# Gate steps moved ahead of the high/low split in the mixture's unit loop, activation loads two units ahead of their split, one extra weight block

## Chip, cores, metric

The kernel runs on one core of one Trainium2 chip. The metric is device time in microseconds of one execution. Before the change the median of 3 runs is 910.09 us (909.3 to 910.9).

## What is computed

Three stages feed each other. A landmark attention (4 batches, 8 heads, 576 positions, head size 64) gives 2304 tokens of 512 features. A wide softplus layer, called the mixture here, follows, and then a layer in which each token goes to one of 8 experts:

```
x  = attention(q, k, v)                                # 2304 x 512
h  = x @ w_in                                          # 2304 x 2048
x  = (maximum(h, 0) + log1p(exp(-abs(h)))) @ w_out     # 2304 x 512
logits = x @ w_gate ; e = argmax(logits)
gate   = softmax(logits)[e] ; eom = 1 / (1 + exp(-(x @ w_output_gate)))
out[t] = gate[t] * eom[t, e] * (maximum(x[t] @ w1[e], 0) @ w2[e])
```

## The kernel before

All matrix products are made in fp32 out of three products of a rounded high part and a low part (high*high, high*low, low*high). So each operand is split once: ScalarE (ACT) copies it to the high part, and VectorE (DVE) subtracts that from the operand to get the low part.

**Stages.** Attention runs from 0 to about 150 us, the mixture from about 136 to 600 us, and the experts from about 592 us to the end. The change lies in the mixture alone.

**Units.** The 2304 tokens are 9 chunks of 256; the 2048 hidden features are 8 pairs of blocks of 128. A *unit* is one pair of hidden blocks for one chunk: 72 units, numbered from 0 in the list `order` (lines 860 to 877). The first 24 (chunks 0, 1 and 2 interleaved) are the *joint stage*, in which the weights are still being prepared; from unit 24 on come chunks 3 to 8, 8 units each. Per unit TensorE (PE) runs `gemm1` (line 635, 24 matmuls into `ps_h`, of which there are two buffers), and then `gemm2` (line 670, 12 matmuls into `acc`) of the unit two before. Between the two stands `softplus` (lines 641 to 661):

- ACT: `t` = abs, `t` = exp, `u`, `l` = ln (lines 649 to 652), then after the sums `gh`, the high part (line 657);
- DVE: the sums `u`, `d`, `l` (lines 654 to 656), then `gl`, the low part (line 659). `d` is the last reader of `ps_h`.

`t`, `u`, `l`, `d` have one buffer each, `gh` and `gl` three.

**Weight steps.** In the joint stage, `units(n)` takes n steps of the generator `weights` (lines 573 to 602). A weight block is 3 steps: the high part on ACT together with the start of the next block's decoding (lines 596, 98), the low part on DVE (line 599), and the rest of the decoding on DVE (lines 100 to 102) with the next load. There are 21 blocks, ordered by when they are needed; `w_in` blocks 12 and 13 (numbers 13 and 14 of the list) are first used by the `gemm1` of unit 16, and 14 and 15 (numbers 17 and 18) by that of unit 19, the odd one of each pair in the second half of its matmuls. Each unit from 1 takes three steps: one after the four ACT operations, one between `gh` and `gl`, one after `gl`. `EXTRA = 0, 5, 8` adds one step at unit 0 and three each at units 5 and 8.

**Activations.** From chunk 3 on, `load_xr` (line 604) loads a chunk's activations by SyncE's (SP's) queue and `split_x` (line 620, through line 107 on ACT and line 108 on DVE) splits them. Both are issued in the same unit: 23 for chunk 3, and the sixth unit of each chunk for the next (line 915).

**Gate steps.** When a chunk's sums are complete, `gate` (line 676) works in ten steps: (1) ACT copies `acc` to `x` (line 679); (3, 5) PE transposes a half (`ps_tr`, line 689) and ACT copies it to `x2t` (line 690); (4, 6) PE makes the logits (`ps_lg`, line 695) and DVE copies them (line 696); (7) eight short DVE operations; (9) the rank, by PE (lines 726, 727), DVE and ACT; (10) DVE, and the store `x_d` by SP (line 751). From unit 27 on two steps are taken per unit: one between `gemm1` and `softplus`, one after `gemm2`. In the last chunk a hook in the middle of each product takes further ones, and after the gate of chunk 7 come the steps of `early` (line 763), which finds the first slots of the expert stage; the first makes `ps_n` (line 767).

The order on every engine is the order in which this code issues (`manual_schedule`, line 853). The unit loop before (the split of the next chunk and the gate's place in it):

```
h = gemm1(p, xs[c], ...)
next(side, None)                    # gate step
gs[i] = softplus(h, units)          # ACT x4, DVE sums, gh, gl
units(...)                          # EXTRA
xs[c + 1] = split_x(load_xr(c + 1)) # p == 5
gemm2(p2, gs.pop(i - LAG), accs[c2])
next(gate) ; next(side, None)       # gate steps
```

Of the kernel before, what the change touches and what calls it, by code (L numbers as in the profile page):

```python
# [12 lines left out]
F32R = DT.float32r  # L13
# [4 lines left out]
ALU = mybir.AluOpType  # L18
# [8 lines left out]
NE, F2 = 8, 1024  # L27
# [3 lines left out]
CH = 256  # L31
NCH = NT // CH
# [9 lines left out]
"""  # L42
NWA = 8
NWO = 3
EXTRA = 0, 5, 8
JOINT = 3
NFIRST = 2
TAIL = 0, 2, 1, 0, 1, 1, 0, 0, 1, 0, 1, 0, 0, 0, 1, 1
# [62 lines left out]
def chain(*gens):  # L111
    for g_ in gens:
        yield from g_
# [3 lines left out]
def moe_nystrom_kernel(ctx: ExitStack, tc: tile.TileContext, q, k, v, w_in, w_out, w_gate, w_ogate, w1, w2,  # L117
                       consts, out):
    nc = tc.nc
# [10 lines left out]
    def cc(name, rows=128):  # L130
        o, n = COFF[name]
        return cst[:rows, o:o + n]
# [313 lines left out]
    osum = gp.tile([128, NTILE + 1, NE], BF16, name="osum")  # L446
    rd = gp.tile([128, NTILE], F32, name="rd")
    rmat = gp.tile([128, NTILE, 128], BF16, name="rmat")
    tri_b = gp.tile([128, 128], BF16, name="tri_b")
    one_b = gp.tile([128, 128], BF16, name="one_b")  # L450
    wg = gp.tile([128, 4, 2 * NE], F32, name="wg")
# [93 lines left out]
    with ExitStack() as mctx:  # L545
# [5 lines left out]
        m3 = pool("m3", 3)  # L551
# [52 lines left out]
        def load_xr(c):  # L604
            if c <= JOINT - 1:
                t = m2.tile([128, 4, CH], F32, tag="x2", name="xr", bufs=3)
                xr = [t[:, :2], t[:, 2:]]
            else:
                xr = [m2.tile([128, 2, CH], F32, tag="deca", name="xr") for _ in range(2)]
            t0 = c * CH  # L610
            while t0 < (c + 1) * CH:
                b, o = divmod(t0, S)
                n = min(S - o, (c + 1) * CH - t0)
                for j in range(2):
                    nc.sync.dma_start(xr[j][:, :, t0 - c * CH:t0 - c * CH + n],
                                      xT_d[b].rearrange("(k p) n -> p k n", p=128)[:, 2 * j:2 * j + 2, o:o + n])
                t0 += n
            return xr

        def split_x(xr):  # L620
            xh = mx_.tile([128, 4, CH], F32R, tag="xh", name="xh")
            xl = mx_.tile([128, 4, CH], F32R, tag="xl", name="xl")
            for j in range(2):
                js = slice(2 * j, 2 * j + 2)
                split_hi_lo(nc, xr[j], xh[:, js], xl[:, js], nc.vector)
            return xh, xl

        def gemm1(p, x, pool=ph, tag="h"):
            ps = pool.tile([128, 512], F32, tag=tag, name="ps_h").rearrange("p (i n) -> p i n", i=2)
            for i in range(2):  # L630
                hi, lo = wcols(whi, 2 * p + i), wcols(wlo, 2 * p + i)
                n = 0
                for kk in range(4):
                    for a, b_ in ((hi, x[0]), (hi, x[1]), (lo, x[0])):
                        nc.tensor.matmul(ps[:, i], a[:, kk], b_[:, kk], start=n == 0, stop=n == 11)  # L635
                        n += 1
                if i == 0:
                    hook()
            return ps

        def softplus(h, units):

            t = sp.tile([128, 2, CH], F32, tag="t", name="t")
            u = sp.tile([128, 2, CH], F32, tag="u", name="u")
            l = sp.tile([128, 2, CH], F32, tag="l", name="l")
            d = sp.tile([128, 2, CH], F32, tag="d", name="d")
            gh = m3.tile([128, 2, CH], F32R, tag="gh", name="gh")
            gl = m3.tile([128, 2, CH], F32R, tag="gl", name="gl")
            nc.scalar.activation(t, h, AF.Abs)
            nc.scalar.activation(t, t, AF.Exp, scale=-1.0)  # L650
            nc.scalar.activation(u, t, AF.Identity, bias=1.0)  # L651
            nc.scalar.activation(l, t, AF.Ln, bias=1.0)
            units(1)
            nc.vector.scalar_tensor_tensor(u, u, -1.0, t, ALU.add, ALU.subtract)  # L654
            nc.vector.scalar_tensor_tensor(d, h, 0.0, u, ALU.max, ALU.subtract)  # L655
            nc.vector.tensor_tensor(l, l, d, ALU.add)  # L656
            nc.scalar.activation(gh, l, AF.Copy)  # L657
            units(1)
            nc.vector.tensor_tensor(gl, l, gh.bitcast(F32), ALU.subtract)  # L659
            units(1)  # L660
            return gh, gl

        def gemm2(p, g, acc):
            for i in range(2):
# [188 lines left out]
        with tc.manual_schedule():  # L853
            xs = {0: x0}
            xr = [load_xr(c) for c in range(1, JOINT)]
            load_w(0)
            gs, accs = {}, {}
            side = iter(())
            np_ = NFF // 2
            order = [(0, p) for p in range(LEAD)]  # L860
            for p in range(np_):
                order += [(0, p + LEAD)] * (p + LEAD < np_) + [(c, p) for c in range(1, JOINT)]
            nj = len(order)
            work = weights()

            HB = {2: (pa, "acc2"), 3: (pb, "tr")}
            fast = [False]

            def hook():
                if fast[0]:  # L870
                    next(side, None)

            def units(n):
                for _ in range(n):
                    next(work, None)

            order += [(c, p) for c in range(JOINT, NCH) for p in range(np_)]
            first = ("acc0", "acc1"), ("acc2", "acc3"), ("tr", "sm")
            for j in (1, 2):
                xs[j] = split_x(xr.pop(0))  # L880
                load_w(j)
            for i in range(len(order) + LAG):
                fast[0] = len(order) - np_ <= i - LAG + 1 < len(order)
                if i == len(order):
                    for _ in side:
                        pass
                    win_ctx.close()
                    rw = ctx.enter_context(tc.tile_pool(name="rw", bufs=1, side="right", reuse_waits="tile"))
                    for j in range(4):
                        raw.append(rw.tile([128, 4, 512], F32, name=f"raw{j}"))  # L890
                    for _ in range(2):
                        ring[0].append([rw.tile([128, 4, 512], F32R, name=f"{n}{len(ring[0]) + 4}") for n in ("hi", "lo")])
                    wk[0] = splits(0, NBASE)
                if i < len(order):
                    c, p = order[i]
                    if i == nj - 1:
                        xr.append(load_xr(JOINT))
                    h = gemm1(p, xs[c], *HB.get(i, ()))
                    if i > nj + LAG:
                        next(side, None)  # L900
                    gs[i] = softplus(h, units if i else int)
                    if i in EXTRA:
                        units(1 if i == 0 else 3)
                    if i == 2:
                        nc.vector.tensor_copy(tri_b, cc("tri"))
                        nc.vector.tensor_copy(one_b, cc("ones"))
                        nc.vector.memset(osum[:, 0], 0.0)
                        nc.vector.tensor_copy(sgn[:, 0], cc("iota")[:1, :NE])
                        nc.vector.tensor_scalar(sgn[:, 1], cc("iota")[:1, :NE], -1.0, None, ALU.mult)
                        for nm, src in ((0, w_gate), (1, w_ogate)):  # L910
                            nc.sync.dma_start(wg[:, :, nm * NE:(nm + 1) * NE], src.rearrange("(k p) e -> p k e", p=128))
                    if i == nj - 1:
                        xs[JOINT] = split_x(xr.pop(0))
                    if p == 5 and JOINT - 1 < c < NCH - 1:
                        xs[c + 1] = split_x(load_xr(c + 1))
                if i >= len(order):
                    xt[i - len(order)] = t_x(i - len(order))
                    wunits(2)
                if i >= LAG:
                    c2, p2 = order[i - LAG]  # L920
                    if p2 == 0:
                        tags = first[c2] if c2 < JOINT else first[c2 % 2]
                        accs[c2] = [(pa if "acc" in t else pb).tile([128, 512], F32, tag=t, name=t) for t in tags]
                    gemm2(p2, gs.pop(i - LAG), accs[c2])
                    if p2 == np_ - 1:
                        ga_ = gate(c2, accs.pop(c2))
                        next(ga_)
                        side = chain(side, ga_)
                        if c2 == NCH - 2:
                            side = chain(side, early())  # L930
                if nj + LAG < i < len(order) + LAG - 1:
                    next(side, None)
            side = chain(side, route())


# [154 lines left out]
```

## Time and profile before

| | |
|---|---|
| median of 3 runs | 910.09 us (909.3 to 910.9) |
| profiled execution, its own time | 910.2 us |
| span of that execution (first to last instruction) | 908.4 us |
| outside the span | 1.8 us |
| PE / DVE / ACT busy in the span | 859.9 / 666.5 / 586.9 us |
| mean granted TensorE clock | 0.988 of full speed |

All durations below come from the one profiled execution. A row of the timeline gives start, duration, engine, line, operation, result and operands; in brackets stands how long the engine was idle before it, and which operation ended that idle time. Matmuls overlap, so their starts say more than their durations.

### The profile page before, as it was taken

What the parts mean: (1) busy time and instruction counts of PE and PEld (TensorE: products, weight loads), DVE (VectorE), ACT (ScalarE), POOL (GpSimd) and SP (SyncE); (2) the same over time, 40 slices, a digit from 0 to 9 for tenths busy, and PEclk for the clock granted to TensorE, in tenths of its full rate; (3) what the DMA queues carried; (4) which work ended last, traced back from release to release, by engine and by line L of the source; (5) the groups of instructions that cost most, each with busy time, mean ns of one, the idle gap of its engine ahead of it and who ended that gap; (6) DMA issues with size and microseconds to landing.
All of it is one profiled execution on the core that took longest, in us unless ns stands there. A gap on an engine that the chain in (4) does not pass through costs nothing.

```text
span 908.4 us, 15419 instructions
## 1 busy us (share of the span) xinstructions
PE 859.9 (95%) x5826; PEld 718.9 (79%) x5826; DVE 666.5 (73%) x1121; ACT 586.9 (65%) x958; POOL 209.5 (23%) x109
## 2 busy tenths in 40 slices
PE   6998987989998999998999998989999999999996
PEld 3665655888997999998899997877888888888885
DVE  0856697999984465556556463668799999999994
ACT  2554565767774655555455554465888888888883
POOL 0001131000000000000000000034666667666662
PEclk9999999999999999999999999999999999999998
DMA  9856555333300000101011000141118369521600
GB/s 222 196 140 183 158 189 166 95 116 97 113 24 24 1 25 1 47 24 47 1 48 47 1 25 1 47 186 59 36 40 292 148 222 366 185 105 35 232 26 33
DMA packets 49516, 90.92 MB, mean 100 GB/s; under 512 B 5471, under 2 KB 32095, under 8 KB 47392
## 3 DMA queue, kind: packets, MB, share of 16 engines
q1 hardware_dynamic: 41408, 74.43, 26.6%
q0 software_dynamic: 3680, 10.78, 3.7%
q10 hardware_dynamic: 4352, 4.72, 1.5%
q8 instruction: 46, 0.75, 0.4%
q14 instruction: 30, 0.25, 0.1%
HBM read 134.46 MB, written 15.48 MB: 165 GB/s over the span
## 4 chain that ended last, share of the span: by engine, by line
PE 68%; DVE 14%; DMA 6%; ACT 6%; issue 4%; POOL 0%; SPq 0%; DVEq 0%; POOLq 0%; ACTq 0%
PE ps_h L635 19%; PE acc L670 15%; PE ps_g L960 10%; PE ps_y L985 9%; DMA raw<-in_moe_w 3%; DVE lo L479 2%; DVE dect L101 2%; PE ps_hT L974 2%; ACT hi L477 2%; PE ps_lg L695 2%; DVE deca L102 1%; PE ps_t L185 1%; PE ps_t L161 1%; DVE l L656 1%; DVE d L655 1%
## 5 line engine op out<-in xcount | busy, mean ns | idle before, releaser
L479 DVE TENSOR_TENSOR lo<-raw,hi 128x1024 fp32r<-128x1024 f32 x129 | 226.3, 1781 | 11.4 <-ACT hi L477 11.1
L477 ACT ACTIVATE hi<-raw 128x1024 fp32r<-128x1024 f32 x176 | 176.9, 1063 | 8.5 <-DMA raw<-in_moe_w 8.1
L635 PE MATMUL ps_h<-xh,whi 128*128 128x256 f32 x512 | 148.1, 289 | 7.7 <-DVE d L655 4.8
L635 PE MATMUL ps_h<-xl,whi 128*128 128x256 f32 x512 | 146.3, 286 | 0.4 <-DVE xl L108 0.4
L635 PE MATMUL ps_h<-xh,wlo 128*128 128x256 f32 x512 | 146.2, 286 | 0.0
L486 POOL DMA_INDIRECT xg<-x_d,gidx x23 | 37.0, 1610 | 444.1 <-ACT t L650 433.1
L479 POOL TENSOR_TENSOR lo<-raw,hi 128x1024 fp32r<-128x1024 f32 x47 | 116.7, 2485 | 35.8 <-ACT hi L477 35.6
L657 ACT ACTIVATE gh<-l 128x512 fp32r<-128x512 f32 x72 | 45.5, 632 | 116.0 <-DVE l L656 116.0
L654 DVE SCALAR_TENSOR_TENSOR u<-u,t 128x512 f32<-128x512 f32 x72 | 49.6, 688 | 83.5 <-ACT u L651 83.4
L635 PEld LDWEIGHTS ps_h<-xh,whi 128*128 128x128 f32 x512 | 99.2, 194 | 13.6 <-DVE d L655 6.1
L670 PE MATMUL acc<-woh,gh 128*128 128x512 f32 x256 | 103.1, 403 | 1.6 <-ACT gh L657 1.6
L670 PE MATMUL acc<-wol,gh 128*128 128x512 f32 x256 | 101.0, 394 | 0.0
L635 PEld LDWEIGHTS ps_h<-xl,whi 128*128 128x128 f32 x512 | 99.2, 194 | 2.2 <-DVE xl L108 0.6
L670 PE MATMUL acc<-woh,gl 128*128 128x512 f32 x256 | 100.8, 394 | 0.0
L635 PEld LDWEIGHTS ps_h<-xh,wlo 128*128 128x128 f32 x512 | 99.4, 194 | 0.0
L659 DVE TENSOR_TENSOR gl<-l,gh 128x512 fp32r<-128x512 f32 x72 | 49.9, 693 | 38.8 <-ACT gh L657 37.0
L985 PE MATMUL ps_y<-hi,woh 128*128 128x512 f32 x184 | 76.7, 417 | 0.2 <-ACT woh L977 0.2
L985 PE MATMUL ps_y<-hi,wol 128*128 128x512 f32 x184 | 73.3, 398 | 1.4 <-DVE wol L978 1.3
L960 PE MATMUL ps_g<-hi,x0l 128*128 128x512 f32 x184 | 73.9, 402 | 0.3
L985 PE MATMUL ps_y<-lo,woh 128*128 128x512 f32 x184 | 72.7, 395 | 0.0
L960 PE MATMUL ps_g<-hi,x0h 128*128 128x512 f32 x184 | 72.1, 392 | 0.0
L960 PE MATMUL ps_g<-lo,x0h 128*128 128x512 f32 x184 | 71.9, 391 | 0.0
(246 smaller groups left out, 1756.6 us busy)
## 6 DMA issues: line engine op xcount, KB each, us to landing
raw<-in_moe_w SPq DMA_DIRECT2D x88, 1024.0 KB
raw<-in_moe_w_in SPq DMA_DIRECT2D x16, 512.0 KB
raw<-in_moe_w_out SPq DMA_DIRECT2D x16, 512.0 KB
x_d<-x SPq DMA_DIRECT2D x9, 514.0 KB
k<-in_k SPq DMA_DIRECT2D x8, 576.0 KB
q<-in_q SPq DMA_DIRECT2D x8, 576.0 KB
v<-in_v SPq DMA_DIRECT2D x8, 576.0 KB
xT_d<-xo ACTq DMA_DIRECT2D x16, 288.0 KB
```

What stands on the lines that cost most here:

```text
L101: nc.vector.scalar_tensor_tensor(t, hi32, -0x80000000, t, ALU.bitwise_and, ALU.bitwise_or)
L477: nc.scalar.activation(w[0][:, us], raw[i][:, us], AF.Copy)
L479: eng.tensor_tensor(w[1][:, us], raw[i][:, us], w[0][:, us].bitcast(F32), ALU.subtract)
L486: nc.gpsimd.indirect_dma_start(out=xg, out_offset=None, in_=src, in_offset=bass.IndirectOffsetOnAxis(ap=gidx[:, s:s + 1], axis=0))
L635: nc.tensor.matmul(ps[:, i], a[:, kk], b_[:, kk], start=n == 0, stop=n == 11)
L654: nc.vector.scalar_tensor_tensor(u, u, -1.0, t, ALU.add, ALU.subtract)
L657: nc.scalar.activation(gh, l, AF.Copy)
L659: nc.vector.tensor_tensor(gl, l, gh.bitcast(F32), ALU.subtract)
L670: nc.tensor.matmul(acc[tt], a[:, i, ts_], b_[f], start=f == 0 and n == 0, stop=f == NFF - 1 and n == 2)
L695: nc.tensor.matmul(pl[:, :2 * NE], xt[tt][:, kk], wg[:, kk], start=kk == 0, stop=kk == 3)
L960: nc.tensor.matmul(ps, a[:, kk], b_[:, kk], start=n == 0, stop=n == 11)
L985: nc.tensor.matmul(y, a[:, kk], b_[:, kk], start=half == 0 and n == 0, stop=half == 1 and n == 11)
```

## The change

`softplus` becomes a generator of four stretches: the four ACT operations, the DVE sums, `gh`, and `gl`. The loop now issues `gemm2` of the unit two before and the gate step behind it between the sums and `gh`. The weight steps keep their three places. `EXTRA` becomes `15, 15, 15`: no extra steps at units 5 and 8, three at unit 15 (unit 0 keeps its one). For chunk 3 the load is issued in unit 21 and the split in unit 22; for later chunks the load is issued in the fourth unit of the chunk before, the split in the sixth, both after the gate's steps.

```diff
-EXTRA = 0, 5, 8
+EXTRA = 15, 15, 15
...
-        def softplus(h, units):
+        def softplus(h):
...
             nc.scalar.activation(l, t, AF.Ln, bias=1.0)
-            units(1)
+            yield
             nc.vector.scalar_tensor_tensor(u, u, -1.0, t, ALU.add, ALU.subtract)
             nc.vector.scalar_tensor_tensor(d, h, 0.0, u, ALU.max, ALU.subtract)
             nc.vector.tensor_tensor(l, l, d, ALU.add)
+            yield
+            gh = m3.tile([128, 2, CH], F32R, tag="gh", name="gh")
+            gl = m3.tile([128, 2, CH], F32R, tag="gl", name="gl")
             nc.scalar.activation(gh, l, AF.Copy)
-            units(1)
+            yield
             nc.vector.tensor_tensor(gl, l, gh.bitcast(F32), ALU.subtract)
-            units(1)
-            return gh, gl
+            yield gh, gl
...
                     c, p = order[i]
-                    if i == nj - 1:
-                        xr.append(load_xr(JOINT))
-                    h = gemm1(p, xs[c], *HB.get(i, ()))
+                    g = softplus(gemm1(p, xs[c], *HB.get(i, ())))
                     if i > nj + LAG:
                         next(side, None)
-                    gs[i] = softplus(h, units if i else int)
-                    if i in EXTRA:
-                        units(1 if i == 0 else 3)
...
-                    if i == nj - 1:
-                        xs[JOINT] = split_x(xr.pop(0))
-                    if p == 5 and JOINT - 1 < c < NCH - 1:
-                        xs[c + 1] = split_x(load_xr(c + 1))
+                    next(g)
+                    if 0 < i < nj:
+                        units(1)
+                    next(g)
...
                 if nj + LAG < i < len(order) + LAG - 1:
                     next(side, None)
+                if i < len(order):
+                    next(g)
+                    if 0 < i < nj:
+                        units(1)
+                    gs[i] = next(g)
+                    if i < nj:
+                        units(1 + EXTRA.count(i))
...
+                    if i == nj - 3 or p == 3 and JOINT - 1 < c < NCH - 1:
+                        xr.append(load_xr(max(c + 1, JOINT)))
+                    if i == nj - 2 or p == 5 and JOINT - 1 < c < NCH - 1:
+                        xs[max(c + 1, JOINT)] = split_x(xr.pop(0))
```

PE issues the same matmuls in the same order in both kernels. Three places show what moves on the other engines.

SP's queue around the load of chunk 6 (`xr`, in pieces of 192 and 64 columns), before and then changed; `x_d` are the gate's stores:

```order
L751 DMA x_d<-x_3665 128x2x514
L751 DMA x_d<-x_4181 128x2x514
L615 DMA xr<-xT_d 128x2x192 x2
L615 DMA xr<-xT_d 128x2x64 x2
L751 DMA x_d<-x_4723 128x2x514
```

```order
L751 DMA x_d<-x_3661 128x2x514
L615 DMA xr<-xT_d 128x2x192 x2
L615 DMA xr<-xT_d 128x2x64 x2
L751 DMA x_d<-x_4177 128x2x514
L751 DMA x_d<-x_4719 128x2x514
```

The load of chunk 6 moves in front of the store of chunk 3's gate.

ACT in units 65 and 66, where the gate of chunk 7 begins, before and then changed (lines 649 to 652 and 657 of before are 647 to 650 and 658 of the change):

```order
L652 ACTIVATE l<-t 128x512 [waits DVE_49]
L657 ACTIVATE gh<-l 128x512 [waits DVE_49]
L679 ACTIVATE x_6256<-acc_5816 128x512 [waits DMAHW3_49,PE_49]
L679 ACTIVATE x_6256<-acc_5817 128x512 [waits PE_49]
L690 ACTIVATE x2t<-ps_tr 128x512 [waits PE_49]
L649 ACTIVATE t<-ps_h 128x512 [waits PE_49,Activation_49]
L650 ACTIVATE t<-t 128x512 [waits Activation_49]
L651 ACTIVATE u<-t 128x512 [waits Activation_49]
L652 ACTIVATE l<-t 128x512 [waits DVE_49]
L657 ACTIVATE gh<-l 128x512 [waits DVE_49]
L690 ACTIVATE x2t<-ps_tr 128x512 [waits PE_49]
```

```order
L650 ACTIVATE l<-t 128x512 [waits DVE_49]
L679 ACTIVATE x_6252<-acc_5812 128x512 [waits DMAHW3_49,PE_49]
L679 ACTIVATE x_6252<-acc_5813 128x512 [waits PE_49]
L658 ACTIVATE gh<-l 128x512 [waits DVE_49]
L690 ACTIVATE x2t<-ps_tr 128x512 [waits PE_49]
L647 ACTIVATE t<-ps_h 128x512 [waits PE_49,Activation_49]
L648 ACTIVATE t<-t 128x512 [waits Activation_49]
L649 ACTIVATE u<-t 128x512 [waits Activation_49]
L650 ACTIVATE l<-t 128x512 [waits DVE_49]
L690 ACTIVATE x2t<-ps_tr 128x512 [waits PE_49]
L658 ACTIVATE gh<-l 128x512 [waits DVE_49]
```

The copies of `acc` (unit 65) and the second `x2t` (unit 66) move in front of `gh`, which waits for DVE's `l`.

DVE in the joint stage at the low part of `w_in` block 13 (number 14 of the list), before (in unit 13) and then changed (in unit 15, with the three extra steps behind it):

```order
L599 TENSOR_TENSOR wlo_2002<-deca,whi_2001 128x4x128
L659 TENSOR_TENSOR gl<-l,gh 128x512
L100 TENSOR_SCALAR dect<-deca 128x512
L101 SCALAR_TENSOR_TENSOR dect<-raw,dect 128x512
L102 SCALAR_TENSOR_TENSOR deca<-raw,dect 128x512
L654 SCALAR_TENSOR_TENSOR u<-u,t 128x512
L655 SCALAR_TENSOR_TENSOR d<-ps_h,u 128x512
```

```order
L599 TENSOR_TENSOR wlo_2002<-deca,whi_2001 128x4x128
L660 TENSOR_TENSOR gl<-l,gh 128x512
L100 TENSOR_SCALAR dect<-deca 128x512
L101 SCALAR_TENSOR_TENSOR dect<-raw,dect 128x512
L102 SCALAR_TENSOR_TENSOR deca<-raw,dect 128x512
L599 TENSOR_TENSOR wol_2070<-deca,woh_2057 128x512
L100 TENSOR_SCALAR dect<-deca 128x512
L101 SCALAR_TENSOR_TENSOR dect<-raw,dect 128x512
L102 SCALAR_TENSOR_TENSOR deca<-raw,dect 128x512
L652 SCALAR_TENSOR_TENSOR u<-u,t 128x512
L653 SCALAR_TENSOR_TENSOR d<-ps_h,u 128x512
```

Numbers 9 to 14 of the list are made two units later than before, 5 to 8 and 15 to 20 one unit later.

## Rows read from the trace of the kernel before

**Rows 1.** The page, part 1: busy time, share of the span, instructions.

```profile
PE 859.9 (95%) x5826; PEld 718.9 (79%) x5826; DVE 666.5 (73%) x1121; ACT 586.9 (65%) x958; POOL 209.5 (23%) x109
```

**Rows 2.** Stretches: length, busy PE, PEld, DVE, ACT, POOL; PEclk; DMA share; GB/s.

```profile
180.00:215.00 35.00, 30.39 (x191) 26.99 (x191) 31.56 (x51) 24.16 (x42) 0.00 (x0) 1.00 0.35 105
272.00:320.00 48.00, 44.75 (x281) 40.47 (x281) 23.12 (x38) 26.82 (x48) 0.00 (x0) 0.96 0.05 12
363.00:410.00 47.00, 47.00 (x322) 43.22 (x321) 27.09 (x65) 25.88 (x46) 0.00 (x0) 1.00 0.10 34
410.00:460.00 50.00, 47.10 (x296) 41.99 (x295) 27.33 (x72) 26.72 (x49) 0.00 (x0) 0.97 0.15 43
```

**Rows 3.** Timeline of PE: rows with an idle gap ahead, 180 to 600 us.

```profile
191.27 0.39 PE L635 MATMUL ps_h<-xh,whi 128*128 128x256 f32 x1 [2.44 <-DVE d L655]
...
210.57 0.39 PE L635 MATMUL ps_h<-xh,whi 128*128 128x256 f32 x1 [2.17 <-DVE d L655]
...
286.73 0.38 PE L635 MATMUL ps_h<-xh,whi 128*128 128x256 f32 x1 [2.83 <-ACT xh L107]
...
430.01 1.07 PE L695 MATMUL ps_lg<-wg,x2t 128*128 128x16 f32 x8 [2.51 <-ACT x2t L690]
...
457.12 0.66 PE L689 MATMUL ps_tr<-cst,x 128*128 128x128 f32 x4 [0.38 <-ACT x L679]
...
553.06 0.66 PE L689 MATMUL ps_tr<-cst,x 128*128 128x128 f32 x4 [1.37 <-ACT x L679]
...
560.61 1.06 PE L695 MATMUL ps_lg<-wg,x2t 128*128 128x16 f32 x8 [1.36 <-ACT x2t L690]
...
572.27 0.17 PE L767 MATMUL ps_n<-osum,one_b 128*128 128x8 bf16 x1 [1.82 <-DVE cd L736]
```

**Rows 4.** Chain that ended last: start, length, piece; two at full clock, two partly at half.

```profile
303.31 2.75 PE acc L670 x12
306.06 2.87 PE ps_h L635 x24
...
431.07 4.31 PE acc L670 x12
...
561.67 4.47 PE ps_h L635 x24
```

**Rows 5.** Timeline of DVE, joint stage: d of units 5, 6, 14, 15; a weight low part.

```profile
181.97 0.69 DVE L655 SCALAR_TENSOR_TENSOR d<-ps_h,u 128x512 f32<-128x512 f32 x1
...
190.52 0.69 DVE L655 SCALAR_TENSOR_TENSOR d<-ps_h,u 128x512 f32<-128x512 f32 x1
...
236.69 0.69 DVE L655 SCALAR_TENSOR_TENSOR d<-ps_h,u 128x512 f32<-128x512 f32 x1
...
238.09 0.68 DVE L599 TENSOR_TENSOR wol<-deca,woh 128x512 fp32r<-128x512 f32 x1
...
242.06 0.69 DVE L655 SCALAR_TENSOR_TENSOR d<-ps_h,u 128x512 f32<-128x512 f32 x1
```

**Rows 6.** Timeline of PE: the start of unit 7's first product.

```profile
183.05 0.28 PE L635 MATMUL ps_h<-x0h,whi 128*128 128x256 f32 x1
```

**Rows 7.** Timeline of SP and ACT at the load and split of chunk 6.

```profile
422.91 0.36 SPq L751 DMA_DIRECT2D x_d<-x  x1
...
423.36 2.44 SPq L615 DMA_DIRECT2D xr<-xT_d  x4
...
428.32 1.15 ACT L107 ACTIVATE xh<-xr 128x512 fp32r<-128x512 f32 x2 [1.60 <-DMA xr<-xT_d]
```

**Rows 8.** Timeline of DVE in the last chunk: a gate operation; gl of unit 67.

```profile
561.92 0.17 DVE L716 TENSOR_REDUCE mx<-lg 128x2 f32<-128x16 f32 x1
...
571.16 0.69 DVE L659 TENSOR_TENSOR gl<-l,gh 128x512 fp32r<-128x512 f32 x1 [0.69 <-ACT gh L657]
```

**Rows 9.** Timeline, unit 34: gl, and the second product's first matmul that needs it.

```profile
358.83 0.69 DVE L659 TENSOR_TENSOR gl<-l,gh 128x512 fp32r<-128x512 f32 x1 [0.70 <-ACT gh L657]
...
365.02 0.40 PE L670 MATMUL acc<-woh,gh 128*128 128x512 f32 x1
```

More of the change, by code (lines that the diff above doesn't have):

```diff
@@ L646, in softplus @@
             d = sp.tile([128, 2, CH], F32, tag="d", name="d")
-            gh = m3.tile([128, 2, CH], F32R, tag="gh", name="gh")
-            gl = m3.tile([128, 2, CH], F32R, tag="gl", name="gl")
             nc.scalar.activation(t, h, AF.Abs)
@@ L895, in moe_nystrom_kernel @@
                     c, p = order[i]
-                    if i == nj - 1:
-                        xr.append(load_xr(JOINT))
-                    h = gemm1(p, xs[c], *HB.get(i, ()))
+                    g = softplus(gemm1(p, xs[c], *HB.get(i, ())))
                     if i > nj + LAG:
                         next(side, None)
-                    gs[i] = softplus(h, units if i else int)
-                    if i in EXTRA:
-                        units(1 if i == 0 else 3)
[L904 to L911, printed above, removed]
-                    if i == nj - 1:
-                        xs[JOINT] = split_x(xr.pop(0))
-                    if p == 5 and JOINT - 1 < c < NCH - 1:
-                        xs[c + 1] = split_x(load_xr(c + 1))
+                    next(g)
+                    if 0 < i < nj:
+                        units(1)
+                    next(g)
                 if i >= len(order):
@@ L932, in moe_nystrom_kernel @@
                     next(side, None)
+                if i < len(order):
[5 more added lines that the diff above has]
+                        units(1 + EXTRA.count(i))
+                    if i == 2:
+                        nc.vector.tensor_copy(tri_b, cc("tri"))
+                        nc.vector.tensor_copy(one_b, cc("ones"))
+                        nc.vector.memset(osum[:, 0], 0.0)
+                        nc.vector.tensor_copy(sgn[:, 0], cc("iota")[:1, :NE])
+                        nc.vector.tensor_scalar(sgn[:, 1], cc("iota")[:1, :NE], -1.0, None, ALU.mult)
+                        for nm, src in ((0, w_gate), (1, w_ogate)):
+                            nc.sync.dma_start(wg[:, :, nm * NE:(nm + 1) * NE], src.rearrange("(k p) e -> p k e", p=128))
+                    if i == nj - 3 or p == 3 and JOINT - 1 < c < NCH - 1:
+                        xr.append(load_xr(max(c + 1, JOINT)))
+                    if i == nj - 2 or p == 5 and JOINT - 1 < c < NCH - 1:
+                        xs[max(c + 1, JOINT)] = split_x(xr.pop(0))
             side = chain(side, route())
```

## The prediction, made before the changed kernel ran

> **What bounds the kernel now.** I read the page first: PE is busy for 95% of the span [rows 1], so time is to be had only where PE stands idle or runs slow. Then the stretches: from 363 to 410 us PE is busy for all 47.00 us, while from 180 to 215 it lacks 4.61 us, from 272 to 320 3.25 us and from 410 to 460 2.90 us [rows 2]. Then the timeline of PE, which names each gap and what ended it [rows 3]. Between 180 and 600 us these are all the places with over 0.3 us: two in the joint stage behind DVE's `d` (2.44, 2.17), one at chunk 3 behind the split (2.83; the whole 3.25 us of that stretch, with a short second wait right behind it), one at 430 behind `x2t` (2.51), one of 0.38 behind a copy of `acc`, and three in the last chunk (1.37, 1.36, 1.82). A unit without a gap takes 2.75 + 2.87 = 5.62 us on PE [rows 4].
>
> **What a gap costs besides itself.** After the gap at 430 the next twelve matmuls took 4.31 us and not 2.75; after that at 560.6 a first product took 4.47 and not 2.87 [rows 4]. That is 1.56 and 1.60 us more, at the lower of the two clock levels, 1.2 instead of 2.4 GHz. The stretch 272 to 320, with the 2.83 us gap, has a granted clock of 0.96 [rows 2], which is 0.04 x 48 = 1.9 us of clock by a rounded figure; I take 1.6. The stretch 180 to 215 with its two gaps stayed at 1.00 [rows 2]. So a gap of 2.5 us may bring a slow stretch or not.
>
> A row and a rule differ here. From 410 to 460 PE's idle time is 2.90 us, but weight loading is busy for 41.99 of 50 us, against 43.22 of 47 where nothing waits [rows 2]; at that rate the stretch has lost 50 - 41.99 x 47/43.22 = 4.3 us. The Trainium skill, "Perfetto Trace Analysis", section "Identifying the Most-Contended Engine", says that matmul busy time is no good measure of the headroom and that the share of weight loading is. By the idle gaps alone the sum below would be 9.7 us, with the slow clock it is 14.5; by that rule the trace sides with the larger.
>
> **Joint stage: no gain.** DVE is the busiest engine there (31.56 of 35 us) [rows 2]. `d` comes every 242.06 - 236.69 = 5.37 us, and 190.52 - 181.97 = 8.55 us across an extra block [rows 5]; PE needs 5.62. So DVE wins 0.25 us per unit on PE, and an extra block costs it 3.2. Before, the block at unit 5 finds no reserve, and neither does that at 8: the two gaps. The change takes both away. `d` of unit 5 ends at 182.66 [rows 5] and unit 7's first product starts at 183.05 [rows 6]; from there the reserve grows to some 2.9 us at unit 15, where one extra block uses it up. That looks like 4.6 us won.
>
> But the weight blocks now come later. Number 14 is made in unit 15 and is needed in the second half of unit 16's first product; 18 in unit 18, needed in unit 19. A block's low part ends 238.77 - 237.38 = 1.39 us after the end of its unit's `d` [rows 5]. The `d` of unit 15 ends at 182.66 + 10 x 5.37 = 236.4, so block 14 is there at 237.8. PE would reach the 15th matmul of unit 16 at 183.05 + 9 x 5.62 + 14 x 0.12 = 235.3. **A new wait of 2.45 us.** The `d` of unit 18 ends 8.55 + 2 x 5.37 later, at 255.7, block 18 at 257.05; PE, 2.45 late, would be there at 183.05 + 12 x 5.62 + 2.45 + 1.68 = 254.6. **A second wait of 2.43 us.** Together 4.88 for 4.61: +0.3 us. A slow stretch after the first would be swallowed by the second, for block 18 sets the time; one after the second would cost 1.6. Bounds: -4.6 (no new wait) and +3 (both waits 0.5 longer, and a slow stretch). I take +0.3. The other blocks are ready in time: number 10 ends 182.66 + 6 x 5.37 + 1.39 = 216.3, and unit 13 wants it at 183.05 + 6 x 5.62 + 1.68 = 218.4.
>
> **Chunk 3's split: -4.85.** Issued in unit 22 and not 23, it runs a unit (5.62 us) earlier on ACT and DVE, and PE's idle time there is 3.25 us [rows 2]; with the slow stretch, 3.25 + 1.6. The load is issued after unit 21's steps, about 11 us ahead of the split's use; the one slow load seen took 428.32 - 423.36 = 5 us from issue to its split [rows 7].
>
> **Chunk 6's load: -4.45.** SP issued it behind the gate's store at 422.91, which waits for DVE; ACT then sat 1.60 us at `xh` [rows 7], and `x2t`, behind it on ACT, held PE for 2.51 [rows 3]. The change puts the load in front of that store and two units ahead of the split, and `x2t` in front of the split. So 2.51 and the slow 1.56 go; so do the 0.38 us at 457, where the copy of `acc` stood behind `gh`. The other loads showed no wait and move with nothing behind them but stores.
>
> **Last chunk: -5.5.** The gaps of 1.37 and 1.36 end when ACT gets to the copy of `acc` and to `x2t` [rows 3], both behind `gh`, which waits for `l`. In front of `gh` they need only PE: both go, with the slow 1.60. The gap of 1.82 waits for DVE's rank step, which stands behind `gl`; `gl` with its wait for `gh` is 0.69 + 0.69 [rows 8]. In the change `gl` comes after that step. Of 1.82 some 0.6 stay (1.82 - 1.38 = 0.44, and a little for the steps of `early`, which DVE cannot start earlier by as much). So 1.37 + 1.36 + 1.2 + 1.6 = 5.5.
>
> **What is pushed back.** `gh` now waits behind ACT's gate copies, which wait for PE, and `gl` behind DVE's gate steps. In a plain unit `gl` ends at 359.52 and is first needed at 365.02 [rows 9], 5.5 us of reserve. The copy of `acc` or `x2t` can start once PE has done 2.75 us of second product [rows 4] and the transposes, about when `l` is ready; the longest gate step puts eight short DVE operations of 0.17 us [rows 8], some 1.4 us, in front of `gl`. ACT's next abs waits for PE's next product anyway. I cost it at nothing; without that cover it would be the 1.4 us of such a unit.
>
> **Sum.** 0.3 - 4.85 - 4.45 - 5.5 = -14.5 us. The profiled execution took 910.2 us, 0.1 above the median of 910.09, so against the median: **895.6 us**. The expert stage starts when the last first product ends and shifts as a whole.
>
> **Rivals.**
>
> - *The new waits in the joint stage cost clock too.* They are as long as the gap that did (2.51) and the one that did not (2.44) [rows 3]. For it: two of them; against: the stage kept clock 1.00 with such gaps [rows 2]. +1.6, and up to 0.5 for each wait: 897 to 899. Chance 0.20.
> - *PE does not wait for the blocks.* The two joint gaps simply go: 895.6 - 4.9 = 890.7. Against it: DVE's 5.37 us rhythm leaves no room. Chance 0.07. The same section of the Trainium skill tells to work on the most contended engine first; that is DVE here by its busy time, and the change takes none of its work away, so by that rule too this rival fails.
> - *Half stays.* The split or the gate's copies meet another wait just behind (the store of a gate held in SP's queue, PSUM of the rank step), and one of the three gains of about 5 us is lost: about 900.5. Chance 0.08.
> - *Slower.* ACT takes its queue in order, so every gate copy in front of `gh` now ties `gh`, `gl` and the next ln (which needs `l`'s one buffer) to PE's second product. It decides if `gl` comes more than a unit (5.62 us) after its time, when ACT and DVE no longer keep PE's rhythm. Priced by the longest step, 1.4 us [rows 8], in two of the five units that each of 7 gates spans: 14 x 1.4 = 19.6 us more, 915. Against it: 5.5 us of reserve [rows 9]. Chance 0.05.
> - *Nothing moves*, since new waits take all back: 910. Chance 0.03.
>
> The forecast has 0.57. It spans 893.5 to 897 (0.5 on each wait, 0.4 on each slow stretch). The range of 8 in 10 takes in the clock rival and half of the third at the top, and the no-wait rival at the bottom: 890.5 to 900.5. A measurement of this kernel can tell about 0.2% (1.8 us) from no change. Faster: all but the last two, 0.92; same 0.03; slower 0.05.
>
> **What would show it.** Gaps of PE at the first products of units 16 and 19, each about 2.4 us, behind DVE's weight low part; none behind `d`. No gap ahead of chunk 3. No ACT wait for `xr`, and no gap at `x2t` or the copies of `acc`. One gap of about 0.6 us at `ps_n`. Slow-clock stretches: from 150 to 600 us none, or one after unit 19. The forecast is wrong if PE waits for `gl` or `gh` anywhere after unit 24, or if the joint stage ends much before or after its old time.

## The result, and the profile after

| | before | after |
|---|---|---|
| median | 909.69 us (908.71 to 910.9, 4 runs) | 896.23 us (895.14 to 896.6, 4 runs) |
| ratio | 1 | 0.9849, 95% interval 0.9832 to 0.9867 |
| profiled execution / its span | 910.2 / 908.4 us | 895.93 / 894.1 us |

The change makes the kernel 13.5 us faster; 895.6 was forecast. In the page, part 1, of the changed kernel, the busy times are those of [rows 1] within 3.2 us for every engine, while the span is 14.3 us shorter. The work is the same; waits and some slow clock have gone.

```profile
PE 856.7 (96%) x5826; PEld 716.9 (80%) x5826; DVE 665.1 (74%) x1121; ACT 587.2 (66%) x958; POOL 209.4 (23%) x109
```

Line numbers in the changed kernel: sums 652 to 654, `gh` 658, `gl` 660, abs 647; from the gate on they are as before. First its stretches (columns as in [rows 2]):

```profile
180.00:215.00 35.00, 35.00 (x225) 31.84 (x224) 32.52 (x53) 26.63 (x46) 0.00 (x0) 1.00 0.31 93
215.00:240.00 25.00, 22.86 (x145) 20.54 (x144) 23.34 (x38) 17.04 (x29) 0.00 (x0) 1.00 0.34 103
240.00:272.00 32.00, 30.07 (x182) 27.09 (x181) 26.05 (x42) 21.85 (x38) 0.00 (x0) 0.95 0.21 60
272.00:320.00 48.00, 48.00 (x315) 43.85 (x315) 24.07 (x40) 30.27 (x53) 0.00 (x0) 1.00 0.06 17
410.00:460.00 50.00, 50.00 (x337) 45.67 (x336) 28.46 (x72) 28.47 (x52) 0.00 (x0) 1.00 0.10 33
```

PE now has no idle time from 180 to 215, from 272 to 320 and from 410 to 460 us, where it lacked 4.61, 3.25 and 2.90 [rows 2]. It lacks 2.14 and 1.93 us in two stretches of the joint stage instead. Then the timeline of PE, all rows with 0.3 us idle ahead or more from 180 to 590 us:

```profile
235.52 0.39 PE L635 MATMUL ps_h<-x0h,whi 128*128 128x256 f32 x1 [0.51 <-ACT whi L596]
237.66 0.38 PE L635 MATMUL ps_h<-x0h,wlo 128*128 128x256 f32 x1 [1.63 <-DVE wlo L599]
254.83 0.39 PE L635 MATMUL ps_h<-x0h,whi 128*128 128x256 f32 x1 [0.30 <-ACT whi L596]
256.96 0.58 PE L635 MATMUL ps_h<-x0h,wlo 128*128 128x256 f32 x1 [1.62 <-DVE wlo L599]
556.94 0.17 PE L767 MATMUL ps_n<-osum,one_b 128*128 128x8 bf16 x1 [0.43 <-DVE cd L736]
561.90 0.24 PE L791 MATMUL ps_i<-erhs,rmat 128*128 128x4 bf16 x4 [0.52 <-DVE erhs L786]
```

All eight rows of [rows 3] are gone but the one at `ps_n`, and that shrank from 1.82 to 0.43. New are the waits for weight blocks in units 16 and 19, 0.51 + 1.63 and 0.30 + 1.62. At `ps_i`, in the last chunk, there is a new wait of 0.52. The chain that ended last shows what the clock took behind the second of the waits for blocks (start, length, piece):

```profile
256.96 2.50 PE ps_h L635 x10
259.46 3.11 PE acc L670 x12
```

The same two pieces behind the same wait (1.63) in a kernel that differs only in when the loads of chunks 4 to 8 are issued (further down), where the stretch 240 to 272 has a granted clock of 1.00:

```profile
256.33 1.45 PE ps_h L635 x10
257.78 2.75 PE acc L670 x12
```

So the lower clock level took 1.05 + 0.36 = 1.41 us, which is in the 0.95 of the stretch 240 to 272. And the idle time is not all that a wait costs: at full clock ten matmuls take 10/24 of 2.87 = 1.20 us [rows 4], but 1.45 behind this wait.

Where the time came from is read from the starts of the units' first products in the two timelines of PE:

| first product of unit | before | after | difference | won or lost since the row above | forecast |
|---|---|---|---|---|---|
| 7 | 183.05 | 182.84 | -0.21 | | |
| 20 (behind the joint waits) | 261.25 | 262.41 | +1.16 | +1.37 | +0.3 |
| 25 (behind chunk 3's split) | 294.65 | 290.51 | -4.14 | -5.30 | -4.85 |
| 48 (behind chunk 6's load) | 442.32 | 433.81 | -8.51 | -4.37 | -4.07 |
| 64 | 538.86 | 529.60 | -9.26 | -0.75 | -0.38 |
| 71 (last chunk) | 588.37 | 573.63 | -14.74 | -5.48 | -5.5 |
| end of the profiled execution | 910.2 | 895.93 | -14.27 | +0.47 | 0 |

On ACT (its timeline), chunk 6's split now follows `gh` with no wait for its load, and in the next unit `x2t` stands in front of `gh` and waits for PE alone:

```profile
421.95 0.63 ACT L658 ACTIVATE gh<-l 128x512 fp32r<-128x512 f32 x1 [0.83 <-DVE l L654]
422.49 1.13 ACT L107 ACTIVATE xh<-xr 128x512 fp32r<-128x512 f32 x2
...
427.48 0.60 ACT L690 ACTIVATE x2t<-ps_tr 128x512 f32<-128x512 f32 x1 [1.53 <-PE ps_tr L689]
427.98 0.62 ACT L658 ACTIVATE gh<-l 128x512 fp32r<-128x512 f32 x1
```

What was pushed back is seen in unit 53, one of those with the least reserve from unit 25 to 69 (unit 61 is 0.04 us tighter). The timelines of DVE and PE, `gl` and the second product's first matmul, before and then changed:

```profile
482.28 0.69 DVE L659 TENSOR_TENSOR gl<-l,gh 128x512 fp32r<-128x512 f32 x1 [0.70 <-ACT gh L657]
...
488.15 0.40 PE L670 MATMUL acc<-woh,gh 128*128 128x512 f32 x1
```

```profile
473.46 0.67 DVE L660 TENSOR_TENSOR gl<-l,gh 128x512 fp32r<-128x512 f32 x1
...
479.04 0.40 PE L670 MATMUL acc<-woh,gh 128*128 128x512 f32 x1
```

`gl` now ends at 474.13, 4.91 us before it is wanted; in the same unit of before it was 5.18. The least of all these units was 4.91 before (unit 62) and is 4.87 now, so the worst case has hardly moved; unit 66, which had 13.03, has 8.46. PE waits for `gl` or `gh` nowhere after unit 24.

### The profile page after: what moved, and what is told of

It reads as the page before. It is cut to its first block, busy times and chain, and to the rows that moved or that the text cites. A ratio compares the mean times of both kernels' runs of the same rounds, so it can differ in the third digit from the quotient of the medians.

```text
span 894.1 us, 15416 instructions
## 1 busy us (share of the span) xinstructions
PE 856.7 (96%) x5826; PEld 716.9 (80%) x5826; DVE 665.1 (74%) x1121; ACT 587.2 (66%) x958; POOL 209.4 (23%) x109
## 4 chain that ended last, share of the span: by engine, by line
PE 69%; DVE 14%; DMA 5%; issue 5%; ACT 4%; POOL 1%; SPq 0%; DVEq 0%; POOLq 0%; ACTq 0%
PE ps_h L635 19%; PE acc L670 16%; PE ps_g L966 10%; PE ps_y L991 9%; DMA raw<-in_moe_w 3%; DVE dect L101 2%; PE ps_hT L980 2%; DVE lo L479 2%; PE ps_lg L695 2%; DVE deca L102 2%; PE ps_t L185 1%; ACT hi L477 1%; PE ps_t L161 1%; PE ps_l L197 1%; DVE d L653 1%
```

## Experiments: what each part is worth

Four kernels ran beside the kernel before, which took 910.64 us there. **The extra block alone**: the kernel before with one line changed.

```
-EXTRA = 0, 5, 8
+EXTRA = 0, 15
```

> The kernel before with only the extra weight blocks changed (none at units 5 and 8, one at unit 15). My theory: the two gaps behind d (2.44 and 2.17 us) go and two waits for a weight block, at the first products of units 16 and 19, come in their place, 2.45 and 2.43 us by the prediction (2.1 and 1.9 in the changed kernel). About 909.7 us, 0 to +1.6 with a slow-clock stretch behind the second. Rival (the gaps simply go): 905.1 us and no wait at units 16 and 19.

Measured: 910.01 us, ratio 0.9991 (0.9976 to 1.0007). No change that can be measured, as the forecast's joint term of +0.3 said: the two gaps behind `d` went, and waits for weight blocks came at unit 16 (0.51 + 1.63) and unit 19 (0.64).

**The loads alone**: the kernel before, with load and split as in the change and `gh` and `gl` where they were.

```
-if i == nj - 1: xr.append(load_xr(JOINT))        # in front of gemm1
-if i == nj - 1: xs[JOINT] = split_x(xr.pop(0))
-if p == 5 and ...: xs[c + 1] = split_x(load_xr(c + 1))
+if i == nj - 3 or p == 3 and ...: xr.append(load_xr(max(c + 1, JOINT)))
+if i == nj - 2 or p == 5 and ...: xs[max(c + 1, JOINT)] = split_x(xr.pop(0))
```

> The kernel before with only the loads and chunk 3's split moved (load two units ahead of the split, chunk 3's split in unit 22); gh, gl and the weight steps stay. My theory: chunk 3's gap with its slow stretch (4.85 us) and chunk 6's (2.51 + 1.56) go, the small gap of 0.38 and those of the last chunk stay: 909.7 - 8.9 = 900.8 us. Rival (the gap at chunk 6 comes from x2t standing behind gh and the split on ACT, not from the late load): only 4.85 goes, 904.8 us, and PE still waits for x2t near 425 us.

Measured: 902.12 us, ratio 0.9913 (0.9889 to 0.9938). The gap at chunk 3 is gone; the one at chunk 6 shrank from 2.51 to 0.81 us. Timelines of ACT and PE in this kernel, where `gh` is line 657:

```profile
420.51 0.63 ACT L657 ACTIVATE gh<-l 128x512 fp32r<-128x512 f32 x1 [1.83 <-DVE l L656]
421.05 1.14 ACT L107 ACTIVATE xh<-xr 128x512 fp32r<-128x512 f32 x2
422.09 0.58 ACT L690 ACTIVATE x2t<-ps_tr 128x512 f32<-128x512 f32 x1
...
422.72 1.06 PE L695 MATMUL ps_lg<-wg,x2t 128*128 128x16 f32 x8 [0.81 <-ACT x2t L690]
```

ACT no longer waits for the load, but `x2t` still stands behind `gh` and the split. So the earlier load takes 1.70 us off that gap, and the place of `x2t` holds the rest (the next kernel shows that this place alone takes off all of it). The gaps of the last chunk stayed.

**The order alone**: the changed kernel with load and split issued in one unit as before and the old extra blocks. Both then stand at the end of that unit, behind `gl` and the gate's steps, so this is not the order quite alone: the loads of chunks 7 and 8 come behind one store more than before.

```
-EXTRA = 15, 15, 15
+EXTRA = 5, 5, 5, 8, 8, 8
-if i == nj - 3 or p == 3 and ...: xr.append(...)    # and the split's line
+if i == nj - 1: ...                                 # chunk 3's load and split, as before
+if p == 5 and ...: xs[c + 1] = split_x(load_xr(c + 1))
```

> Only the new place of gh and gl (behind the second product and the gate step); loads issued with the split as before, chunk 3's split in unit 23, extra blocks at units 5 and 8. My theory: the last chunk's gaps go (5.5 us with the slow stretch), and chunk 6's gap too (4.45), since x2t now stands in front of the split though the load is still late; chunk 3's gap stays: 909.7 - 9.9 = 899.8 us, with an ACT wait of 1 to 2 us for xr near 424 us that PE does not feel. Rival (the late load holds PE all the same): 903.9 us. If the split late in the unit holds chunk 3 longer than before, up to 1 us more.

Measured: 905.28 us, ratio 0.995 (0.9933 to 0.9966), 5.5 us above what I expected. Chunk 6's gap went whole, though ACT still waits 0.92 us for its load; the last chunk's gaps shrank. What I had not seen are two new gaps behind `d` (0.72 and 0.89 us), and that 0.88 and 0.38 stay at a copy of `acc` and at `x2t`: 2.87 us, most of the 3.5 by which the profiled execution (903.33 us) lies above what I expected. The first new one in the timelines of SP, ACT and PE:

```profile
477.76 0.36 SPq L751 DMA_DIRECT2D x_d<-x  x1
478.22 1.34 SPq L615 DMA_DIRECT2D xr<-xT_d  x2
...
481.97 1.34 ACT L107 ACTIVATE xh<-xr 128x512 fp32r<-128x512 f32 x2 [4.69 <-DMA xr<-xT_d]
...
486.79 0.36 PE L635 MATMUL ps_h<-xh,whi 128*128 128x256 f32 x1 [0.72 <-DVE d L653]
```

The load of chunk 7 is here behind the store of chunk 5's gate in SP's queue, and the store waits for DVE; before, it was behind that of chunk 4 (453.64). The split is the last thing that ACT does in the unit, so ACT stands 4.69 us, the next unit's abs and exp come late, DVE's `d` with them, and PE waits. The second new gap follows in the same way from 4.93 us of ACT at chunk 8's load, and ACT has not caught up when the gate of chunk 7 begins: its abs of unit 65 starts 5.13 us after that unit's first product, against 3.13 in the changed kernel. That fits the two gaps that stay, but no run tests it. So the later place of the split needs a load that is not pushed behind the next gate's store.

**Everything but the extra block**: the changed kernel with the old blocks.

```
-EXTRA = 15, 15, 15
+EXTRA = 5, 5, 5, 8, 8, 8
```

> The changed kernel with the extra weight blocks back at units 5 and 8. My theory: the joint stage is bound by DVE's work either way, two gaps of 2.4 and 2.2 us behind d instead of 2.1 and 1.9 behind weight blocks: within 1.6 us of the changed kernel (896.2), so 894.5 to 897. Rival (moving the block was worth its two gaps): 4 to 5 us slower than the changed kernel, 900.5 us.

Measured: 895.38 us, ratio 0.9842 (0.982 to 0.9863): the whole gain without the extra block's move. Its timeline of PE has the two gaps behind `d` of before and no wait for a weight block:

```profile
191.53 0.39 PE L635 MATMUL ps_h<-xh,whi 128*128 128x256 f32 x1 [2.42 <-DVE d L653]
...
210.84 0.39 PE L635 MATMUL ps_h<-xh,whi 128*128 128x256 f32 x1 [0.68 <-DVE d L653]
```

The second is 0.68 and not 2.17, because the lower clock followed the first (0.83 from 190 to 200 us, where it was 1.00 before): PE comes to it later by as much. So waits alone do not tell what the stage costs; the time from the first product of unit 7 to that of unit 20 does. It is 78.20 us before, 78.18 here and 78.17 with the extra block alone.

So the loads and chunk 3's split give 8.5 us by the medians, the order 5.4 beside later loads, the two together 15.3, and the move of the extra block nothing that can be measured. No kernel moved `gh` without `gl`; what each is worth in the last chunk is not shown.

## Experiments: the split's place, and how early the load has to be

The kernel before took 910.17 us beside these two and the two with POOL below. **Chunk 3's split alone back to unit 23**, with its load still at unit 21:

```
-if i == nj - 2 or p == 5 and ...:   # split
+if i == nj - 1 or p == 5 and ...:
```

> The changed kernel with chunk 3's split alone put back from unit 22 to unit 23, behind that unit's gl; its load stays at unit 21. Theory: the split's place on ACT made the gap in front of unit 24, not the load: it comes back at 2.83 + 0.42 us, with 1.6 us of half clock behind it: 896.2 + 4.85 = 901.1 us (899 to 902). Rival: the load's lateness made it, and with the load early the split at unit 23 is hidden: 896.2 us.

Measured: 900.06 us, ratio 0.9892 (0.9869 to 0.9916), outside the changed kernel's interval by little, and outside that of the next kernel, which ran beside it. Timeline of PE and the stretch 272 to 320:

```profile
286.89 0.38 PE L635 MATMUL ps_h<-xh,whi 128*128 128x256 f32 x1 [2.83 <-ACT xh L107]
287.69 0.39 PE L635 MATMUL ps_h<-xl,whi 128*128 128x256 f32 x1 [0.42 <-DVE xl L108]
...
272.00:320.00 48.00, 44.74 (x293) 40.53 (x292) 23.77 (x38) 27.39 (x48) 0.00 (x0) 1.00 0.05 12
```

The gap of before came back to the hundredth with its load early, so the split's place made it. By the medians the price is 3.8 us above 896.23, not 4.85. In this profile no lower clock followed (1.00): the five units from 20 to 25 take 31.88 us, against 28.10 in the changed kernel and 33.40 before. So 3.25 us of idle time cost 3.78, and the lower clock of before 1.52.

**Chunks 4 to 8 loaded one unit ahead instead of two**:

```
-if i == nj - 3 or p == 3 and ...:   # load
+if i == nj - 3 or p == 4 and ...:
```

> The changed kernel with the loads of chunks 4 to 7 one unit in front of their split instead of two. The only transfers that change their order are chunk 6's, which now stand behind the store of 417.3 us instead of in front of it; they would be issued from about 417.7 to 420.2 us and land near 422.5 us, against a split near 424 us. Theory: one unit is enough where the split stands in front of the next unit's work, 896.2 us (895 to 897.5). Rival: a load behind the store lands too late, ACT waits for it and chunk 6's logits with it, at most the 4.45 us that the prediction gave for chunk 6: 898 to 900.7 us.

Measured: 895.89 us, ratio 0.984 (0.9817 to 0.9863): no difference. First the timeline of SP at chunk 6's load. In that of ACT its split waits 0.49 us for it, and PE has no gap there. The last row is the stretch 240 to 272 of the comparison above:

```profile
415.33 0.36 SPq L751 DMA_DIRECT2D x_d<-x  x1
415.79 2.48 SPq L615 DMA_DIRECT2D xr<-xT_d  x4
...
421.03 1.15 ACT L107 ACTIVATE xh<-xr 128x512 fp32r<-128x512 f32 x2 [0.49 <-DMA xr<-xT_d]
...
240.00:272.00 32.00, 30.07 (x190) 27.02 (x189) 26.70 (x43) 23.40 (x42) 0.00 (x0) 1.00 0.23 66
```

From chunk 4 on, every load stands here behind the same store as in the kernel before: chunk 6's behind that of chunk 3's gate, as in [rows 7]. So beside the new order the loads of these chunks need not move in front of any store. What costs time is the place behind the next gate's store that the order alone gave to chunks 7 and 8. One unit is enough for that, and the second unit of the change gains nothing; chunk 3's split is another matter.

## Experiments: can the joint stage's last 4 us be had?

**The low part of a weight block on POOL**, which is idle there, instead of DVE:

```
-nc.vector.tensor_tensor(lo, a, hi.bitcast(F32), ALU.subtract)
+nc.gpsimd.tensor_tensor(lo, a, hi.bitcast(F32), ALU.subtract)
```

> The changed kernel, but the low part of a weight block in the joint stage is taken on POOL instead of DVE; POOL is idle there (0.00 us busy between 180 and 272 us), DVE is busy 23.3 of 25 us between 215 and 240 us. Theory: the two waits left in the joint stage (2.14 us in front of unit 16, 1.92 us in front of unit 19) come from DVE's rate, a low part is 0.69 us of DVE per unit; with it gone both waits go, with the 1.7 us of the half-clock stretch behind the second: 896.2 - 4.06 - 1.7 = 890.5 us (889.5 to 892.5). Rival 1: the waits come from the order of the steps (a block is finished one unit before it is used, whatever DVE's rate), and POOL's low part takes 1.36 us instead of 0.69: each wait grows by about 0.7 us, 897.6 us (896.5 to 899). Rival 2: POOL's use makes DVE's own rows longer, so that the gap returns behind d: 896 us or more.

Measured: 904.9 us, ratio 0.9936 (0.9915 to 0.9957). My theory was 14 us off. Timelines of DVE and POOL in this kernel, unit 9:

```profile
207.07 0.69 DVE L653 SCALAR_TENSOR_TENSOR d<-ps_h,u 128x512 f32<-128x512 f32 x1
207.86 1.10 DVE L654 TENSOR_TENSOR l<-l,d 128x512 f32<-128x512 f32 x1
209.66 0.69 DVE L660 TENSOR_TENSOR gl<-l,gh 128x512 fp32r<-128x512 f32 x1 [0.70 <-ACT gh L658]
...
213.71 1.10 DVE L654 TENSOR_TENSOR l<-l,d 128x512 f32<-128x512 f32 x1
...
207.10 1.31 POOL L599 TENSOR_TENSOR wol<-deca,woh 128x512 fp32r<-128x512 f32 x1 [4.54 <-ACT woh L596]
```

The timeline of DVE in the same unit of the changed kernel:

```profile
204.05 0.69 DVE L654 TENSOR_TENSOR l<-l,d 128x512 f32<-128x512 f32 x1
204.66 0.68 DVE L599 TENSOR_TENSOR wol<-deca,woh 128x512 fp32r<-128x512 f32 x1
205.44 0.69 DVE L660 TENSOR_TENSOR gl<-l,gh 128x512 fp32r<-128x512 f32 x1
...
209.43 0.69 DVE L654 TENSOR_TENSOR l<-l,d 128x512 f32<-128x512 f32 x1
```

There the low part fills exactly the 0.7 us in which `gl` must wait for `gh`. Taken out, it leaves DVE idle for 0.70 us, so nothing is saved; and `l` takes 1.10 instead of 0.69 us while POOL works. From one `l` to the next it is 213.71 - 207.86 = 5.85 us against 209.43 - 204.05 = 5.38. PE needs 5.62, so DVE has turned from 0.24 us ahead per unit to 0.23 behind. Unit 20 starts at 270.53 instead of 262.41, 8.1 us later: about all of the loss. By the rhythm 3.7 us of it are there when unit 16 starts (237.16 against 233.43). The other 4.4 come in unit 16, whose waits are 3.02 + 0.57 instead of 0.51 + 1.63, with the clock at 0.50 behind them from 242 to 247 us. The second rival named the right engine, but not that the saving itself was nil.

**The same with two extra blocks, at units 6 and 12** (`EXTRA = 6, 6, 6, 12, 12, 12`):

> As the kernel with the low parts on POOL, with the extra blocks' steps two at unit 6 and unit 12 instead of one at unit 15, so every block is finished earlier. By DVE's rate as the cause: 890.5 us (889.5 to 892.5), the same as with the one extra block at unit 15, since DVE is no longer full. If the order of the steps is the cause: the waits go here and only here, 890.5 us here against about 897.6 us there. If POOL slows DVE: gaps behind d at the units after 6 and 12, 895 us or more.

Measured: 903.53 us, ratio 0.9931 (0.9911 to 0.995). No wait for a weight block is left, but gaps of 3.81 and 3.56 us behind `d` follow the extra blocks. First products stand 5.85 us apart again from unit 15 to 20: DVE has no reserve.

The kernel before took 910.23 us beside the last four. **The changed kernel again**:

> The changed kernel once more, for comparison with the other kernels of this call: 896.2 us (895 to 897), with waits of 0.51 + 1.63 us for unit 16's weight block and 0.3 + 1.6 us for unit 19's.

Measured: 895.47 us, ratio 0.9838 (0.9814 to 0.9862), with the same waits of 0.53 + 1.63 and 0.31 + 1.63.

**The extra block's three steps at three units, one each**:

```
-EXTRA = 15, 15, 15
+EXTRA = 5, 8, 11
```

> The changed kernel with the one extra block's three steps at units 5, 8 and 11, one step each, instead of all three at unit 15. Theory: in the joint stage a unit is 5.62 us of PE against a loop of 5.38 us through DVE, so DVE gains 0.24 us on PE in each unit; spread out, the steps' 2.5 us of DVE (0.69 + 0.42 + 0.69 + 0.69) meet the reserve three times instead of once, and the block is early, so that the waits of 2.14 and 1.92 us go: gaps of 1 to 2 us behind d are left of 4.06, and no stretch of half clock behind them: 893.5 us (892 to 895.5). Rival: the extra work is 2.5 us of DVE wherever it stands and the reserve is used up by then; the waits turn into gaps behind d of the same sum: 896 us (895 to 897).

Measured: 904.33 us, ratio 0.9934 (0.9912 to 0.9957), 8.9 us slower than the kernel just above. Both theories fall, for both counted DVE's work and not its order. Timelines of DVE and ACT between units 7 and 8 of this kernel:

```profile
201.83 0.69 DVE L102 SCALAR_TENSOR_TENSOR deca<-raw,dect 128x512 int32<-128x512 int32 x1
202.44 0.68 DVE L660 TENSOR_TENSOR gl<-l,gh 128x512 fp32r<-128x512 f32 x1
...
205.60 0.69 DVE L652 SCALAR_TENSOR_TENSOR u<-u,t 128x512 f32<-128x512 f32 x1 [1.68 <-ACT u L649]
...
202.56 0.64 ACT L596 ACTIVATE woh<-deca 128x512 fp32r<-128x512 f32 x1 [1.16 <-DVE deca L102]
...
203.65 0.58 ACT L647 ACTIVATE t<-ps_h 128x512 f32<-128x512 f32 x1
```

A unit has three places for weight steps and a block has three steps, so each step meets the same place in every unit. One step more shifts that: now the decoding stands where the low part stood, and the block's high part stands on ACT in front of the next abs. It waits 1.16 us for the decoding, and DVE then waits 1.68 for ACT. The first products of PE stand 7.15 us apart instead of 5.62, with gaps of 2.41, 1.25, 1.27 and 1.28 us behind `d`, until the second extra step changes the order again. Unit 16's wait is gone, but unit 19's grows to 1.72 + 1.63.

**The same at units 8, 11 and 13**:

> The changed kernel with the extra block's steps at units 8, 11 and 13, one each. By the theory that a spread block is paid from DVE's 0.24 us per unit: later steps find more reserve than at 5, 8 and 11, gaps of 0.5 to 1.5 us, 893 us (891.5 to 895). By the rival that the work is paid in full wherever it stands: 896 us (895 to 897).

Measured: 903.54 us, ratio 0.9923 (0.99 to 0.9946): again gaps of 1.67, 1.27, 1.27 and 1.34 us behind `d`, and a wait of 1.78 + 1.64 for unit 19's block. The shift costs the same later.

**One whole extra block, at unit 5**:

```
-EXTRA = 15, 15, 15
+EXTRA = 5, 5, 5
```

> The changed kernel with the one extra block at unit 5 instead of unit 15. Theory: one gap of 2.4 us behind d at unit 8, as with two extra blocks, and unit 16's wait gone; unit 19's is answered by the same block, so it goes too: 4.06 - 2.4 = 1.6 us less, 894.6 us (893.5 to 896). Rival: a block at unit 5 serves unit 16 alone and unit 19's 1.92 us stays: 896.4 us (895.5 to 898).

Measured: 894.7 us, ratio 0.9833 (0.9808 to 0.9859), which can't be told from the 0.9838 of the changed kernel. Its timeline of PE:

```profile
191.21 0.39 PE L635 MATMUL ps_h<-xh,whi 128*128 128x256 f32 x1 [2.43 <-DVE d L653]
...
257.14 0.39 PE L635 MATMUL ps_h<-x0h,wlo 128*128 128x256 f32 x1 [0.66 <-DVE wlo L599]
```

Unit 16's wait is gone. Unit 19's stays, as the rival said, but shows as 0.66 and not 1.92, since PE comes to it late: the clock fell behind the gap of 2.43 (0.50 from 193 to 196 us), and the wait takes that in. From unit 7 to unit 20 it is 78.19 us. With whole extra blocks and the low part on DVE, wherever the blocks stood (one early, one late, two early), this time is 78.17 to 78.21 in eight profiles, the one before among them. Only the two of the changed kernel, where the lower clock fell behind the last wait and nothing after it could take it in, have 79.57 and 79.66. No placement tried beat the changed kernel measurably.

## Why the prediction was right

**The reading of PE's gaps** carried it. Each gap was named with the operation that ended it and the reason why that was late, and each reason was tested: the split's place (its move back restores 2.83 + 0.42), `x2t` and the copies of `acc` behind `gh` (gone with the order), and the load of chunk 6 behind the store, which turned out not to matter beside the new order.

**Joint stage**, forecast +0.3. The mechanism was right: the new waits stand at units 16 and 19, behind the low part, at 2.14 and 1.92 us where 2.45 and 2.43 were worked out from DVE's rhythm, and with the loads one unit ahead, at full clock, the stage costs what it cost before (78.18 against 78.20). But the first rival came in as well: lower clock followed the second wait, 1.41 us, and the term measured +1.37. That a slow stretch behind the first wait would be swallowed by the second was right too: in the kernel with the extra block alone and in that with chunk 3's split put back, unit 16 took 9.84 and 9.81 us instead of 8.27, unit 19's wait shrank to 0.64 and 0.67, and the stage took 78.17 and 78.18.

**Chunk 3**, forecast -4.85, measured -5.30 to unit 25. The clock's part was about right, 1.52 where 1.6 was taken. The gap was priced too low: 3.25 us of idle time cost 3.78, for the first matmuls behind a gap take longer than those in a stream (with the split put back, the 23 behind the second wait took 3.01 us at full clock, where 23/24 of 2.87 is 2.75).

**Chunk 6**, forecast -4.45, measured -4.37 to unit 48 and -0.75 to unit 64 with the copy of `acc`: -5.12. The idle time and the clock in it were sized right, and what they leave out is again of the size seen behind other gaps. The forecast named two moves for it without parting them, and gave the term to the load. The runs part them: `x2t` in front of `gh` and the split removes the gap with the load still late, the load alone leaves 0.81.

**Last chunk**, forecast -5.5, measured -5.48. `ps_n` kept 0.43 of the 0.6 allowed, and a new wait of 0.52 stands at `ps_i`, later in `early`. Idle time and clock alone would have given 1.37 + 1.36 + 1.39 + 1.60 - 0.52 = 5.20, so the match to 0.02 is partly luck.

**The cover of `gl`**: costed at nothing, rightly; the least reserve is 4.87 us, against 4.91 before.

The errors (-0.21, +1.07, -0.45, -0.67, +0.02, and +0.47 after unit 71) sum to +0.23 in the profile: +1.56 against -1.33. That they offset each other is luck; the total is better than its terms.

The rival without waits for the blocks fell, and the Trainium skill's rule beside it ("Perfetto Trace Analysis", "Identifying the Most-Contended Engine": work on the engine that is busy most) needs care here: DVE is the busiest of its kind, yet taking 0.69 us per unit from it saved nothing, since the way from `l` through ACT's `gh` to `gl` is as long without that work, and giving it to POOL cost 8.7 us. The share of weight loading, which that section prefers for PE, behaved as the prediction used it: 45.67/50 = 0.913 in a stretch without a wait, 0.920 in [rows 2].

## What to carry to other kernels

Name, for every gap of the bound engine, what ended it and what stood in front of that operation in its own queue; the repair is often an exchange of places there, and its worth is the gap, a little more for the first matmuls behind it, and the slow clock if one follows. Compare placements by the time between two fixed points and not by the sum of the waits, for a wait takes in what was lost before it. Before taking work off a busy engine, look at what it covers: work that fills the wait for another engine is free, and moving it saves nothing. Where side work is interleaved with a loop at fixed places, add whole periods of it, for a part of one shifts all that follows.

## What was not expected of the hardware

POOL's 1.31 us subtraction made DVE's `l`, with two operands in SBUF, take 1.10 instead of 0.69 us, while `d`, with one operand in PSUM, took its 0.69 over the same POOL instruction. The Trainium skill says why ("SBUF — State Buffer", "SBUF: two separate sides"): GpSimd shares a port pair with VectorE, which a VectorE instruction with two SBUF inputs needs too, and the later one waits. The rows agree with it roughly: POOL's instruction ends at 208.41 and `l` 0.55 us behind it.

The lower clock is not tied to a gap's length alone. The same waits at units 16 and 19 were followed by 0.95 in 240 to 272 us in the changed kernel and by 1.00 with the load one unit ahead, and chunk 3's gap of 2.83 us by 0.96 before [rows 2] and by 1.00 with the split put back. What decides it stays open; in these two pairs it is worth 1.4 and 1.5 us, close to what a measurement of this kernel can tell.
